# Talking-heads attention with two feed-forward layers: f32 scores by head pairs from TensorE transposes, a second mixer in quarter-array products, and one planned pool of four two-bank PSUM places

## Chip, cores, metric

The kernel runs on one core of a Trainium2 chip. The metric is the device time of one execution in microseconds, the median of several runs; the time before is 1440.85 us (three runs, 1440.46 to 1446.3).

## The reference

```python
# q, k, v: (4, 12, 448, 64) f32; w_pre, w_post: (12, 12)
scores = q @ k^T / 8                                     # per batch and head, 448 x 448
scores = einsum("bhij,hg->bgij", scores, w_pre)          # first mixer: over the heads
attn   = softmax(scores, axis=-1)
attn   = einsum("bhij,hg->bgij", attn, w_post)           # second mixer
x      = (attn @ v), heads side by side                  # 1792 x 768
h = x @ w_in;  x = (h * cos(h)) @ w_out                  # 768 -> 2048 -> 768
h = x @ w_in2; out = (relu(h) ** 2) @ w_out2             # 768 -> 2048 -> 768
```

## The kernel before

All work is recorded first, as operations of a `Plan` (L27 to L128). Each operation has the engines that may do it with a cost for each, a key from the table `KEYS`, the operations that it follows, and the buffers that it takes and gives back (`acq`, `rel`, counted in `room`). A list scheduler then fixes at build time which engine does what and in which order every engine issues; SP issues nearly all DMAs, in its own order. So a changed cost, key or buffer count moves instructions all over the program.

**Stages of a batch.** q and k come in as `raw`, 112 rows with four sequence positions each, by DMAs whose runs are 1 KB (`load_ops`, L522). Outside the first chunk their squares give norms, and the scaled values are split into two f16 halves (`x1`, `x2`, `x3`), which 16-bit DMA transposes (L629, eight a batch) bring into stacks with the head dimension on the partitions; swap copies (L639, L640) make the second stack of k. The queries are handled in chunks `CHUNKS = (0,11), (110,12), (230,12), (348,10)`: first query and number of blocks of 10 queries, 45 blocks a batch. For each chunk and head two f16 matmuls (`scores_ops`, L702) give scores in one bank `s`; ACT (L710) or DVE (L712) copies them to `sh`, and a DMA (L715) moves them into `t`, where a row is a query and a head. Only the first chunk of batch 0 takes another way: f32 transposes on TensorE (L747, L748, L772), f32 scores (L796) and moves by L824.

**A pair of blocks** then goes through the mixers (22 pairs and one single block a batch, 88 steps in all). First mixer, L874: 5 queries of 12 heads are 60 rows, so each block is two quarter products of 64x64 weights with 448 columns, the pair four quarters, in a two-bank place `m`. DVE takes the row maxima of both (L882), ACT the exponential of each block with its row sum (L890), then POOL and DVE the reciprocals (L902). For each block `g` is the block-diagonal weight matrix times the reciprocals, 128x120 (ACT L250 or DVE L248). Second mixer, L924: for each block four products, each with 112 keys of the exponentials as weights and the 120 columns of `g`, into one bank `po`, which ACT (L945) or DVE (L947) copies to `at`, keys on the partitions. After a chunk the value product (L995) multiplies `at` by v, 48 matmuls of 112 rows in two column halves, in `po` banks too; L1018 and L1029 keep the result as a sum of two 16-bit parts.

PSUM is divided into one bank for `s`, two places of two banks for `m`, and three banks for `po` (`PSB`), which the feed-forward layers use as well: gemm 1 (L1334, `h_a`) puts two of three column groups into an `m` place and the third into a `po` bank.

A name in the rows is a buffer of the program (`s`, `m`, `po`, `av` as above, `tk` and `tq` the transposes of the first chunk, `h_a` gemm 1 of the first layer).

## Time and profile before

| what | value |
|---|---|
| median of three runs | 1440.85 us |
| profiled execution, its time | 1443.57 us |
| profiled execution, its span | 1441.8 us |
| PE (TensorE matmul) busy | 1335.2 us, 93% |
| DVE busy | 959.8 us, 67% |
| ACT busy | 764.4 us, 53% |
| POOL busy | 451.3 us, 31% |

The span runs from the first to the last instruction of the profiled execution; 1.8 us of its time lie outside. The profiled execution is 2.7 us above the median. Shares are of the whole span; the stages differ much in them, and the rows below go by stage. An f32 product shows as two records in the rows, an f16 product and a transpose as one. PEclk is the mean clock granted to TensorE, as a share of its full speed.

### The profile page before, as it was taken

The page shows a single profiled execution, that of the slowest core. Times are in us where ns is not written, and L with a number is a line of the kernel's source. Part 1 is how long each engine was busy: PE and PEld are TensorE (multiplying, and loading weights), DVE is VectorE, ACT ScalarE, POOL GpSimd, SP SyncE. Part 2 cuts the span into 40 slices and gives each one's busy share as a digit, 9 for nine tenths or more (in the row PEclk, how much of TensorE's full clock was granted, in tenths as well). Part 3 has the DMA queues.
Part 4 walks back from the last instruction along what each step waited for, and adds up shares of the span by engine and source line. Part 5 has one row for each costly group of instructions (what it writes and reads, how often), then busy time and mean ns, then how long its engine had stood idle before and what let it go on. Part 6 is the DMA issues. An engine that isn't in the chain of part 4 may idle for free.

```text
span 1441.8 us, 26180 instructions
## 1 busy us (share of the span) xinstructions
PE 1335.2 (93%) x10025; PEld 886.0 (61%) x10025; DVE 959.8 (67%) x1968; ACT 764.4 (53%) x1602; POOL 451.3 (31%) x443
## 2 busy tenths in 40 slices
PE   7679888998988999998999999999986999999998
PEld 4356655765766765554455555556864976986965
DVE  5478757665668879987996886988983460461510
ACT  5478677767657747655543543654752440450620
POOL 5023102401401115632642552556361240140300
PEclk7789998999999999999899999999998999999999
DMA  8958884974757558231224133177973440541501
GB/s 170 240 166 215 199 211 143 191 175 132 153 140 196 164 204 215 59 80 53 83 83 132 61 95 125 63 220 224 333 232 117 164 144 23 168 161 44 189 17 28
DMA packets 184445, 209.51 MB, mean 145 GB/s; under 512 B 50828, under 2 KB 165888, under 8 KB 183296
## 3 DMA queue, kind: packets, MB, share of 16 engines
q1 hardware_dynamic: 184224, 207.82, 50.8%
q8 instruction: 79, 1.29, 0.4%
q14 instruction: 46, 0.38, 0.1%
q0 software_dynamic: 96, 0.01, 0.0%
HBM read 123.48 MB, written 29.10 MB: 106 GB/s over the span
## 4 chain that ended last, share of the span: by engine, by line
PE 71%; DVE 12%; DMA 7%; ACT 4%; issue 3%; POOL 1%; SPq 1%; ACTq 0%; DVEq 0%; POOLq 0%
PE h_a L1334 15%; PE o L1920 14%; PE y L1434 12%; PE h_b L1725 8%; PE po L924 7%; PE m L874 4%; DMA t<-sh 4%; PE hx_b L1725 3%; PE s L702 3%; PE av L995 3%; DMA rawin<-in_moe_w_in 2%; DVE mx L882 1%; DVE raw L258 1%; DVE raw L338 1%; ACT e L890 1%
## 5 line engine op out<-in xcount | busy, mean ns | idle before, releaser
L1434 PE MATMUL y<-g,wout 128*128 128x448 f16 x1152 | 225.5, 355 | 4.4 <-ACT g L1345 2.3
L1334 PE MATMUL h_a<-x,win 128*128 128x448 f16 x1152 | 223.9, 354 | 0.5 <-DVE k L1406 0.5
L1725 PEld LDWEIGHTS <-win 128*128 128x128 f16 x2016 | 194.9, 99 | 17.4 <-issue 15.1
L1920 PE MATMUL o<-wout,g 128*128 128x384 f16 x1152 | 191.8, 328 | 0.1
L924 PEld LDWEIGHTS po<-g,e 128*112 128x112 f32 x1440 | 163.1, 179 | 30.3 <-ACT g L250 8.2
L1434 PEld LDWEIGHTS <-wout 128*128 128x128 f16 x1152 | 112.8, 99 | 109.1 <-issue 7.5
L924 PE MATMUL po<-g,e 128*112 128x120 f32 x1440 | 171.7, 271 | 7.1 <-ACT g L250 4.1
L1334 PEld LDWEIGHTS <-win 128*128 128x128 f16 x1152 | 112.8, 99 | 105.3 <-issue 3.6
L1920 PEld LDWEIGHTS <-g 128*128 128x128 f16 x1152 | 113.5, 99 | 74.2 <-issue 2.4
L702 PE MATMUL s<-k,q 128*120 128x448 f16 (+2 forms) x360 | 108.7, 386 | 29.2 <-ACT sh L710 19.5
L1725 PE MATMUL h_b<-win 128*128 128x224 f16 x1152 | 123.9, 261 | 4.2 <-DVE win L1750 4.1
L890 ACT ACTIVATE e<-m,mx 128x448 f32<-128x448 f32 x180 | 112.2, 633 | 23.8 <-DVE mx L882 22.9
L882 DVE TENSOR_REDUCE mx<-m 128x2 f32<-128x896 f32 (+1 forms) x92 | 97.0, 1065 | 39.7 <-PE m L874 38.8
L1936 DVE SCALAR_TENSOR_TENSOR ob<-o,cols,raw 128x384 f32<-128x384 f32 x28 | 17.2, 616 | 147.8 <-PE o L1920 147.8
L874 PE MATMUL m<-t,kmix 64*64 64x448 f32 x704 | 93.0, 615 | 13.6 <-ACT e L890 8.3
L897 POOL TENSOR_SCALAR rs<-sm 128x2 f32<-128x2 f32 (+1 forms) x72 | 16.6, 231 | 283.8 <-ACT e L890 237.5
L1750 DVE TENSOR_TENSOR win<-h_b,win 128x224 f32<-128x224 f32 x128 | 48.6, 389 | 72.0 <-PE h_b L1725 50.1
L702 PEld LDWEIGHTS <-q 128*120 128x120 f16 (+2 forms) x360 | 41.6, 136 | 84.5 <-issue 77.7
L1892 POOL TENSOR_TENSOR r<-r 128x448 f32<-128x448 f32 x25 | 24.1, 964 | 198.3 <-ACT r L1769 198.2
L995 PE MATMUL av<-at,v 112*64 112x120 f32 (+2 forms) x1536 | 80.5, 262 | 5.6 <-ACT at L945 2.7
L995 PEld LDWEIGHTS av<-at,v 112*64 112x64 f32 x1536 | 74.2, 137 | 15.3 <-ACT at L945 5.4
L1350 POOL TENSOR_TENSOR g<-k,g 128x448 f16<-128x448 f32 x52 | 63.4, 1227 | 55.4 <-ACT g L1345 34.0
(310 smaller groups left out, 2225.1 us busy)
## 6 DMA issues: line engine op xcount, KB each, us to landing
win<-wp SPq DMA_DIRECT2D x32, 768.0 KB
raw<-in_moe_w_out SPq DMA_DIRECT2D x21, 1024.0 KB
t<-sh SPq DMA_DIRECT2D x96, 210.0 KB
win<-wp SPq DMA_DIRECT2D x32, 576.0 KB
raw<-in_moe_w_in SPq DMA_DIRECT2D x16, 768.0 KB
wp<-raw SPq DMA_DIRECT2D x8, 1344.0 KB
t<-sh SPq DMA_DIRECT2D x48, 192.5 KB
t<-sh SPq DMA_DIRECT2D x48, 175.0 KB
```

What stands on the lines that cost most here:

```text
L702: PE.matmul(ps[:m, :S], lhsT=lt, rhs=stacks["k"][z][:, h], start=(z == 0), stop=(z == 1))
L874: PE.matmul(st.ps[64 * x : 64 * x + 64, r, :S], lhsT=km[rows, 64 * r : 64 * r + 64], rhs=t[rows, st.blk[x]], start=True, stop=True,)
L882: DVE.tensor_reduce(st.mx[:, :n], st.ps[:, :n, :S], axis=AX.X, op=ALU.max, negate=True)
L890: ACT.activation(st.e[:, x], st.ps[:, x, :S], AF.Exp, bias=st.mx[:, x : x + 1], accum_out=st.sm[:, x : x + 1],)
L924: PE.matmul(o, lhsT=st.e[:, x, c], rhs=st.g[:, x], start=True, stop=True)
L995: PE.matmul(ps[64 * x : 64 * x + 64, gp * 120 : gp * 120 + n], lhsT=v32[:CP, g, jc * D : (jc + 1) * D], rhs=ao[:CP, jc, g, :n], start=(jc ...
L1334: PE.matmul(hb[nm, x], lhsT=t_["win"][:, x, wh, c, :], rhs=xt[b][:, c, xh], start=(c == 0 and wh == 0 and xh == 0), stop=(c == NCC - 1 and ...
L1350: (POOL if e == "POOL" else DVE).tensor_tensor(t_["g"][:, f, 1], box["k"], t_["g"][:, f, 0], op=ALU.subtract)
L1434: PE.matmul(box["ps"][:, :S], lhsT=t_["wo1"][m // 3][:, wh, f, (m % 3) * P : (m % 3 + 1) * P], rhs=t_["g"][:, f, gh], start=(f == 0 and wh ...
L1725: PE.matmul(box[at], lhsT=wt[:, k % 4, wh, c, :], rhs=y(c, xh), start=(first and c == 0 and wh == 0 and xh == 0), stop=(c == HC - 1 and wh ...
L1750: DVE.tensor_tensor(box["s"][:, to], box[at], box["s"][:, k], op=ALU.add)
L1920: PE.matmul(box["ps"][:, :HD], lhsT=(t_["g"][:, f, gh, t0 : t0 + P] if t0 + P <= S else rest()[:, f, gh]), rhs=t_["wo2"][:, 6 * hf : 6 * h ...
```

## The change

- **Loads.** q and k of a batch come by pairs of heads, the two heads of a pair side by side, in runs of 256 bytes (`load_ops`, L533, L535): 24 DMAs in batch 0, 16 in the others. v is padded to 128 rows and comes in eight DMAs (L558).
- **Transposes.** Norms, f16 halves, DMA transposes and swaps are gone, and the special first chunk too. For each pair of heads TensorE does eight f32 transposes (L580) into a two-bank place `tr`, and ACT (L590) or DVE (L592) copies 896 columns into `qk`.
- **Scores.** For each chunk and pair of heads two f32 matmuls of 64 rows, one in each row half of the array (L647), one copy of 896 columns (L655, L657), two moves (L661).
- **Second mixer.** For a pair of blocks 28 products of 64x64 weights and 60 columns, each in a quarter of the array (L747): 5 queries of 12 heads are kept apart, so the zero half of the block-diagonal `g` is not multiplied, and a pair's `g` is one multiplication (L733). Keys come in seven groups of 64, and one instruction (L775, L777) copies a pair's result to `at`.
- **Value product.** Per chunk 72 products over 128 keys and 24 over the last 64, in one two-bank place (L836, L846). The moving operand is read with a stride of five f32 elements.
- **PSUM.** One pool of four two-bank places; the planner assigns the place (`plan.slots["m"]`). Transposes, scores, both mixers, value product and the feed-forward layers all take from it, with a limit of two places on the first mixer (`pm`) and on the pairs of gemm 1 (`h`). Gemm 1 takes pairs throughout.
- **Keys.** All of `KEYS` changes; `SLOTS` spreads the pieces of w_in over three buffers.

```diff
--- before.py
+++ after.py
     KEYS = {
-        "pm": (-188.38, -3899.06, 1478.43, -349.17),
...
+        "pm": (-2.47, -3.04, -3.36, -2.62),
-    PSB = (1, 3)
-    SLOTS = (1, 2, 1, 2, 1, 2, 1, 2, 2, 2, 0, 0, 0, 0, 0, 0)
+    SLOTS = (1, 2, 3, 1, 2, 3, 2, 3, 2, 3, 2, 3, 3, 3, 0, 0)
...
-    ps_s = ctx.enter_context(tc.tile_pool(name="ps_s", bufs=PSB[0], space=PSUM))
-    ps_m = ctx.enter_context(tc.tile_pool(name="ps_m", bufs=2, space=PSUM))
-    ps_o = ctx.enter_context(tc.tile_pool(name="ps_o", bufs=PSB[1], space=PSUM))
+    ps_m = ctx.enter_context(tc.tile_pool(name="ps_m", bufs=1, space=PSUM))
...
+    plan.slots["m"] = list(range(4))
...
+    def banks(nm):
+        i = plan.now["slot"]["m"]
+        return ps_m.tile([P, 2, 512], F32, tag=f"m{i}", name=nm)
     def bank(nm):
-        return ps_o.tile([P, 512], F32, tag="po", name=nm)
+        return banks(nm)[:, 0]
...
+        def load_ops(b, key, step, seq=()):
+            last, done = seq, []
+            for hp in range(0, NP, step):
+                outs = []
+                for nm, src in (("q", q), ("k", k)):
+                    parts = [(z, c) for z in range(2) for c in (range(NC4) if step > 1 else [None])]
+                    for z, c in parts:
+                        def go(e, nm=nm, src=src, z=z, c=c, hp=hp):
+                            if (b, nm) not in raw:
+                                raw[b, nm] = new_raw((b, nm)).rearrange(
+                                    "p (h c x) -> p h c x", h=NP, c=NC4
+                                )
+                            to = raw[b, nm][:CP, hp : hp + step, :, 64 * z : 64 * z + 64]
+                            hs = src[b, 2 * hp + z : 2 * (hp + step) : 2].rearrange(
+                                "h (p c) d -> p h c d", c=NC4
+                            )
+                            if c is None:
+                                SP.dma_start(out=to[:, 0], in_=hs[:, 0])
+                            else:
+                                SP.dma_start(out=to[:, :, c], in_=hs[:, :, c])
...
+        def value_loads(b, key, seq=()):
...
-        def transpose_ops(b, nm, key, dkey, norm):
...
-                def turn(e, g=g):
-                    SP.dma_start_transpose(
-                        out=stacks[nm][0][:, 3 * g : 3 * g + 3].rearrange(
-                            "p h (c x) -> p (h c) x", x=CP
-                        ),
-                        in_=box[g][:CP].rearrange("p h x -> p (h x)"),
-                    )
-                    stage.append(box["n", g])
-                def swap(e, g=g):
-                    t, o = (x[:, 3 * g : 3 * g + 3] for x in stacks[nm])
-                    SP.dma_start(out=o[0:D], in_=t[D:P])
-                    SP.dma_start(out=o[D:P], in_=t[0:D])
...
+        qk = stk.tile([P, NP, 2, S], F32, name="qk")
+        def turn_ops(b, keys, loads):
+            outs, last = [], None
+            for hp in range(NP):
+                box = {}
+                def turn(e, hp=hp, box=box):
+                    ps = box["ps"] = banks(f"tr{b}_{hp}")
+                    for i, nm in enumerate("qk"):
+                        for c in range(NC4):
+                            PE.transpose(
+                                ps[:, i, c * CP : (c + 1) * CP], raw[b, nm][:CP, hp, c],
+                                ident[:CP, :CP],
+                            )
+                    if hp == NP - 1:
+                        raw_done((b, "q"))
+                        raw_done((b, "k"))
+                def keep(e, hp=hp, box=box):
+                    if e == "ACT":
+                        ACT.activation(qk[:, hp], box["ps"][:, :, :S], AF.Copy)
+                    else:
+                        DVE.tensor_copy(qk[:, hp], box["ps"][:, :, :S])
                 last = add(
...
-        def scores_ops(b, ch, h, key, stacked, before):
+        def scores_ops(b, ch, hp, key, turned, before):
             i0, nb = CHUNKS[ch]
             m = nb * IB
             box = {}
             def mm(e):
-                if h == 0:
+                if hp == 0:
                     tt[b, ch] = tts[ch % 2]
-                ps = ps_s.tile([P, 512], F32, tag="s", name=f"s{b}_{ch}_{h}")
-                box["ps"] = ps
-                lt = stacks["q"][0][:, h, i0 : i0 + m]
+                ps = box["ps"] = banks(f"s{b}_{ch}_{hp}")
                 for z in range(2):
+                    r = slice(64 * z, 64 * z + 64)
                     PE.matmul(
-                        ps[:m, :S], lhsT=lt, rhs=stacks["k"][z][:, h], start=(z == 0), stop=(z == 1)
+                        ps[:m, z, :S], lhsT=qk[r, hp, 0, i0 : i0 + m], rhs=qk[r, hp, 1],
+                        start=True, stop=True,
                     )
...
-        def first_chunk_ops(key, dkey, loads):
...
-            def postmix(x):
-                def go(e):
-                    if st.blk[x] == 0:
-                        at[b, ch] = atp.tile([P, 4, H, 12 * IB], F32, tag="at", name=f"at{b}_{ch}")
-                    ps = bank(f"po{st.nm}_{x}")
-                    for jc in range(4):
-                        c = slice(jc * CP, (jc + 1) * CP)
-                        o = ps[:CP, jc * HB : (jc + 1) * HB]
-                        PE.matmul(
-                            o, lhsT=st.e[:, x, c], rhs=st.g[:, x], start=True, stop=True
...
+            W = HB // 2
+            def postmix(e):
+                if st.blk[0] == 0:
+                    at[b, ch] = atp.tile([P, 7, H, 60], F32, tag="at", name=f"at{b}_{ch}")
+                ps = st.po = banks(f"po{st.nm}")
+                def product(rows, bank_, c, at_, r, jt):
+                    PE.matmul(
+                        ps[64 * c : 64 * c + 64, bank_, at_ : at_ + W],
+                        lhsT=st.e[64 * rows : 64 * rows + 64, r, 64 * jt : 64 * jt + 64],
+                        rhs=st.g[64 * rows : 64 * rows + 64, r], start=True, stop=True,
+                    )
+                if n == 2:
+                    for r in range(2):
+                        for jc in range(3):
+                            for x in range(2):
+                                for c in range(2):
+                                    product(x, x, c, (3 * r + jc) * W, r, 2 * jc + c)
+                    for x in range(2):
+                        for r in range(2):
+                            product(x, x, r, 6 * W, r, 6)
...
-            def mm(g0, ng):
-                def go(e):
-                    ao = at[b, ch]
-                    ps = bank(f"av{b}_{ch}_{g0}")
-                    for gp in range(ng):
-                        for jc in range(4):
+            def mm(e):
+                ao = at[b, ch]
+                ps = box["ps"] = banks(f"av{b}_{ch}")
+                def out(gp, x, r):
+                    return ps[64 * x : 64 * x + 64, r, gp * w : (gp + 1) * w]
+                for gp in range(NP):
+                    for jc in range(3):
+                        for r in range(2):
                             for x in range(2):
-                                g = 2 * (g0 + gp) + x
+                                g = 2 * gp + x
                                 PE.matmul(
-                                    ps[64 * x : 64 * x + 64, gp * 120 : gp * 120 + n],
-                                    lhsT=v32[:CP, g, jc * D : (jc + 1) * D],
-                                    rhs=ao[:CP, jc, g, :n],
-                                    start=(jc == 0), stop=(jc == 3),
+                                    out(gp, x, r), lhsT=v32[:, g, jc * D : (jc + 1) * D],
+                                    rhs=ao[:, 3 * r + jc, g, :w].rearrange("p (k m) -> p m k", m=HI),
+                                    start=(gp + jc == 0), stop=False, skip_group_check=True,
                                 )
...
+                for gp in range(NP):
                     for r in range(2):
...
-            if f % 3 == 1:
+            if f % 2:
                 return None
-            fs = [f] if f % 3 or f == NF - 1 else [f, f + 1]
...
-            return add("PE", 3400 * len(fs), key, go, deps, acq=["po" if f % 3 else "m"])
+            return add("PE", 3400 * len(fs), key, go, deps, acq=["m", "h"])
```

Two places of the order that follows from it. The first is PE's, in batch 0, while the second chunk goes through the mixers and the third chunk's scores are made. The digits in a name are batch, chunk, pair, and for `po` before the block; xN counts equal instructions in a row. Before:

```order
L924 MATMUL po0_1_1_0_1015<-g0_1_1_995,e0_1_1_952 112x120 x4
L924 MATMUL po0_1_1_1_1026<-g0_1_1_995,e0_1_1_952 112x120 x4
L702 LDWEIGHTS q0_180
L702 MATMUL s0_2_9_1036<-k0_181,q0_180 120x448
L702 LDWEIGHTS q0_180
L702 MATMUL s0_2_9_1036<-k1_182,q0_180 120x448
L874 MATMUL m0_1_4_1041<-t1_119,kmix0_382 64x448 x4
L874 MATMUL m0_1_5_1052<-t1_119,kmix0_382 64x448 x4
```

And the changed kernel's PE at the same place, where the scores are named by their pair of heads:

```order
L747 MATMUL po0_1_0_915<-g0_1_0_889,e0_1_0_759 64x60 x28
L647 MATMUL s0_2_5_953<-qk_152 120x448 x2
L701 MATMUL m0_1_4_962<-t1_113,kpre_111 64x448 x4
L747 MATMUL po0_1_1_970<-g0_1_1_893,e0_1_1_767 64x60 x28
L701 MATMUL m0_1_5_1006<-t1_113,kpre_111 64x448 x4
L747 MATMUL po0_1_2_1016<-g0_1_2_903,e0_1_2_884 64x60 x28
L647 MATMUL s0_3_0_1048<-qk_152 100x448 x2
L580 MATMUL tr1_0_1058<-ident_69,raw1q_345 128x112 x4
L580 MATMUL tr1_0_1058<-ident_69,raw1k_369 128x112 x4
```

A pair's second mixer is one stretch of 28 small products where two stretches of four stood, the scores have no weight loads written apart, and the transposes of the next batch's pairs now stand between them on PE.

The second place is SP's queue at the start, from its ninth row on, with the DMAs that the first chunk (`t0`) needs. Before:

```order
L629 DMA_TRANSPOSE q0_180<-x2_66 128x12x112
L824 DMA t0_118<-sh00_0_262 10x11x448
L629 DMA_TRANSPOSE k0_181<-x2_66 128x12x112
L824 DMA t0_118<-sh00_0_262 10x11x448
L629 DMA_TRANSPOSE q0_180<-x2_66 128x12x112
L629 DMA_TRANSPOSE k0_181<-x3_67 128x12x112
L824 DMA t0_118<-sh00_1_324 10x11x448 x2
L639 DMA k1_182<-k0_181 64x1344
L640 DMA k1_182<-k0_181 64x1344
```

The changed kernel's SP queue, from its seventeenth row on:

```order
L533 DMA raw0k_167<-in_k 112x4x64 x2
L558 DMA v32_109<-in_v 112x12x64
L558 DMA v32_109<-in_v 16x12x64
L558 DMA v32_109<-in_v 96x12x64
L558 DMA v32_109<-in_v 32x12x64
L558 DMA v32_109<-in_v 80x12x64
L558 DMA v32_109<-in_v 48x12x64
L558 DMA v32_109<-in_v 64x12x64
L661 DMA t0_112<-sh0_0_4_295 10x11x448 x2
L558 DMA v32_109<-in_v 64x12x64
L319 DMA x1_65<-in_moe_w_in 128x6x256
L661 DMA t0_112<-sh0_0_5_319 10x11x448 x2
```

The transposes and swaps that stood between the moves are gone; the loads of q and k (24 of them, the last ones seen here) and seven pieces of v now stand ahead of the last four of the twelve moves.

## Rows read from the trace of the kernel before

**Rows 1.** Busy time of each engine (with instructions) by stretches of the span.
```profile
core 0: us, PE busy (x) PEld busy (x) DVE busy (x) ACT busy (x) POOL busy (x), PEclk, DMA share, GB/s
0.00:58.40 58.40, 38.73 (x187) 22.49 (x187) 26.07 (x66) 24.53 (x46) 19.19 (x26) 0.77 0.89 188
58.40:531.00 472.60, 422.26 (x4042) 298.81 (x4044) 341.12 (x822) 337.34 (x854) 101.45 (x145) 0.95 0.69 174
531.00:1441.80 910.80, 874.17 (x5802) 564.70 (x5798) 592.62 (x1080) 402.58 (x702) 330.62 (x272) 0.98 0.40 127
550.00:1000.00 450.00, 439.33 (x2339) 230.16 (x2338) 381.26 (x637) 236.04 (x373) 222.94 (x172) 0.98 0.35 106
```

**Rows 2.** Waits of PE, 58.4 to 531 us: total, times, longest (us).
```profile
PE s L702 <- ACT sh L710: 17.9, 20, 2.7
PE m L874 <- ACT e L890: 8.3, 9, 1.9
```

**Rows 3.** Instruction groups, 58.4 to 531 us: busy us, mean ns | idle before, releasers.
```profile
L924 PE MATMUL po<-g,e 128*112 128x120 f32 x1440 | 171.7, 271 | 7.1 <-ACT g L250 4.1 <-DVE g L248 1.3 <-DVE at L947 0.6
...
L874 PE MATMUL m<-t,kmix 64*64 64x448 f32 x352 | 92.6, 614 | 13.6 <-ACT e L890 8.3 <-DMA t<-sh 4.7 <-issue 0.5
...
L702 PE MATMUL s<-k,q 128*120 128x448 f16 x178 | 55.9, 399 | 25.1 <-ACT sh L710 16.6 <-DVE sh L712 7.5 <-DVE mx L882 0.7
...
L995 PE MATMUL av<-at,v 112*64 112x120 f32 x768 | 42.5, 268 | 2.0 <-DVE at L947 1.7 <-ACT at L945 0.3
...
L702 PE MATMUL s<-k,q 128*100 128x448 f16 x96 | 26.8, 361 | 0.6 <-DVE sh L712 0.4
...
L702 PE MATMUL s<-k,q 128*110 128x448 f16 x72 | 21.1, 376 | 1.3 <-ACT sh L710 1.3
...
L995 PE MATMUL av<-at,v 112*64 112x110 f32 x384 | 19.8, 260 | 2.4 <-ACT at L945 1.3 <-ACT x L500 0.8 <-DVE at L947 0.4
...
L995 PE MATMUL av<-at,v 112*64 112x100 f32 x344 | 16.3, 251 | 1.1 <-ACT at L945 1.1
```

**Rows 4.** Timeline, 250 to 275 us: start, busy us, engine, line, tile, records.
```profile
251.09 0.15 PEld L874 LDWEIGHTS m<-t,kmix 64*64 64x64 f32 x4 [0.22 <-issue]
...
252.84 3.50 PE L995 MATMUL av<-at,v 112*64 112x120 f32 x64
...
256.78 0.21 PEld L874 LDWEIGHTS m<-t,kmix 64*64 64x64 f32 x8 [0.34 <-issue]
256.78 0.98 PE L874 MATMUL m<-t,kmix 64*64 64x448 f32 x8
...
269.22 1.80 PE L924 MATMUL po<-g,e 128*112 128x120 f32 x16
```

**Rows 5.** Timeline of PE, 0 to 62 us: a group of transposes, the first premix.
```profile
25.00 0.96 PE L772 MATMUL tk<-ident,raw0k 112*128 112x112 f32 x8
...
58.45 3.26 PE L874 MATMUL m<-t,kmix 64*64 64x448 f32 x16 [4.24 <-DMA t<-sh]
```

**Rows 6.** DMA, 0 to 12 us: packets, MB, share of 16 engines.
```profile
q1 hardware_dynamic: 2423, 2.38, 89.2%
```

**Rows 7.** DMA, 20 to 36 us: sizes of all packets; q1 as in rows 6.
```profile
DMA packets 7980, 2.93 MB, mean 183 GB/s; under 512 B 7454, under 2 KB 7850, under 8 KB 7978
...
q1 hardware_dynamic: 7978, 2.90, 105.6%
```

**Rows 8.** Groups of the engines behind the first mixer and the scores.
```profile
L890 ACT ACTIVATE e<-m,mx 128x448 f32<-128x448 f32 x180 | 112.2, 633 | 23.8 <-DVE mx L882 22.9 <-DVE ein L231 0.2
L882 DVE TENSOR_REDUCE mx<-m 128x2 f32<-128x896 f32 x88 | 94.6, 1085 | 39.7 <-PE m L874 38.8
...
L890 ACT ACTIVATION_READ_ACCUMULATOR e<-m,mx 128x1 f32 x180 | 36.8, 204 | 0.0
...
L710 ACT ACTIVATE sh<-s 120x448 f32<-120x448 f32 x52 | 28.2, 542 | 27.9 <-PE s L702 17.0 <-DMA t<-sh 6.3 <-issue 2.6
```

**Rows 9.** Gemm 1 of the first feed-forward layer, the page's costliest groups.
```profile
L1334 PE MATMUL h_a<-x,win 128*128 128x448 f16 x1152 | 223.9, 354 | 0.5 <-DVE k L1406 0.5
```

More of the change, by code (lines that the diff above doesn't have):

```diff
@@ new lines, in value_loads, with go @@
+        def value_loads(b, key, seq=()):
+            outs, last, at_ = [], seq, 0
+            src = v[b].rearrange("h (p c) d -> p c h d", c=NC4)
+            parts = []
+            while at_ < S:
+                n = min(P - at_ % P, CP - at_ % CP)
+                parts.append((at_ % P, at_ // P, at_ % CP, at_ // CP, n))
+                at_ += n
+            parts.append((64, 3, CP - 64, 3, 64))
+            for p0, jc, t0, c, n in parts:
+                def go(e, p0=p0, jc=jc, t0=t0, c=c, n=n):
@@ L720, in scores_ops @@
             o = add(
-                "PE", 380, key, mm, stacked[h // 3] + [before],
-                acq=["s"] + (["t"] if h == 0 else []),
-                rel=[f"{nm}{h // 3}" for nm in "qk"] if ch == 3 and h % 3 == 2 else [],
+                "PE", 760, key, mm, [turned[hp], before],
+                acq=["m"] + (["t"] if hp == 0 else []), rel=[f"qk{hp}"] if ch == 3 else [],
             )
             l = add(
-                {"ACT": 460, "DVE": 570}, 0, key, copy, [o], acq=["sh"], rel=["s"], alone=True
+                {"ACT": 950, "DVE": 1060}, 0, key, copy, [o], acq=["sh"], rel=[("m", o)], alone=True
@@ L853, in attention @@
+            return o, [
+                add("SP", 850, key, move(z), [l], rel=["sh"] * z, dma=10 * m) for z in range(2)
+            ]
         at = {}
@@ new lines, in mixed, with copy @@
+            def mixed(e):
+                ao, i = at[b, ch], st.blk[0] * HI
+                def copy(to, x):
+                    if e == "ACT":
+                        ACT.activation(to, x, AF.Copy)
+                    else:
+                        DVE.tensor_copy(to, x)
+                if n == 2:
+                    copy(
+                        ao.rearrange("p q g i -> p (q g) i")[:, :, i : i + IB].rearrange(
+                            "p a (x m) -> p x a m", x=2
+                        ),
+                        st.po[:, :, : 7 * W].rearrange("p x (a m) -> p x a m", m=HI),
+                    )
+                else:
+                    copy(
+                        ao[:, :6].rearrange("p (r q) g i -> p r (q g) i", r=2)[:, :, :, i : i + HI],
+                        st.po[:, :, : 3 * W].rearrange("p r (a m) -> p r a m", m=HI),
+                    )
+                    for r in range(2):
+                        h = slice(64 * r, 64 * r + 64)
+                        copy(
+                            ao[h, 6, :, i : i + HI],
+                            st.po[h, r, 3 * W : 4 * W].rearrange("p (a m) -> p a m", m=HI),
+                        )
@@ new lines, in view, with got, hi, lo @@
+            def view(z):
+                return xt[b][:, :, z, i0 : i0 + n].rearrange("p g (r i) -> p r g i", r=2)
+            def got():
+                return box["ps"][:, :, : NP * w].rearrange("p r (g i) -> p r g i", g=NP)
+            def hi(e):
+                ACT.activation(view(0), got(), AF.Copy, scale=inv_v[b][:, 0:1])
+            def lo(e):
+                for x in range(2):
+                    DVE.scalar_tensor_tensor(
+                        view(1)[:, x], got()[:, x], inv_v[b][:, 0:1], view(0)[:, x],
+                        op0=ALU.mult, op1=ALU.subtract,
+                    )
@@ L1046, in spaced @@
+            o = add(
+                "PE", 4900, key, mm, [before] + lows + vready[0] + x_free[b], acq=["m"],
+                rel=["at"] + (["v"] if ch == 3 else []),
+            )
+            h = add("ACT", 850, key + 0.1, hi, [o] + vready[1])
+            x_fin[b].append(add("DVE", 1100, key + 0.15, lo, [h], rel=[("m", o)], alone=True))
+            return o
         def spaced(nm, n):
```

626 lines of the change are left out of this document (192 added, 434 removed).

## The prediction

> **What bounds the kernel now.** I read first the busy time of each engine stretch by stretch [rows 1]. Up to 58.4 us TensorE computes for 38.7 us at a mean clock of 0.77 while the DMA engines are 89% busy: the kernel is being loaded. From 58.4 to 531 us, the rest of attention, PE is busy for 422.3 of 472.6 us (89%), DVE and ACT for 341 and 337 (72% each), the DMA engines 69%. From 531 us on, the two feed-forward parts, PE is busy for 874 of 911 us (96%). So past the start PE is the bound, and a change has to shorten its work. What PE waits for in attention is small and scattered: its largest two waits are 17.9 and 8.3 us out of 50 [rows 2]. The groups of PE's work in that stretch [rows 3] say where its time is: the second mixer (L924) 171.7 us, the first mixer (L874) 92.6, the scores (L702) 55.9 + 26.8 + 21.1 = 103.8, the value product (L995) 42.5 + 19.8 + 16.3 = 78.6. They sum to 446.7 against 422.3 us busy, since neighbouring matmuls overlap; I carry the ratio 0.945 along.
>
> **How long a small f32 matmul lasts.** This price carries the sum. An f32 product stands in the rows as two records. Sixteen records of L924 (120 columns, 112 of 128 rows) take 1.80 us, and eight of L874 (448 columns, four 64x64 quarters of the array at once) take 0.98 us [rows 4]. One f16 record of 448 columns lasts 0.36 to 0.40 us [rows 3]; eight such one after another would be 3 us. So the four quarters run side by side, and 0.98 is two passes: 0.37 to the start of the second, and the 0.61 that a record lasts. L924's records last 0.27 us; with the last one off, the other fifteen go by (1.80 - 0.27) / 15 = 102 ns each at 120 columns, thus about 53 ns at 60. The value product's 64 records, alternating between two column halves, take 3.50 us: 54.7 ns a record, half of 109, so two at a time also works there.
>
> **The change part by part, steady attention.** *Second mixer.* Now per pair of blocks 8 products, 16 records in series. Then 28 quarter products of 60 columns, 56 records in seven rounds of four, each two passes: 14 x 53 ns + 0.27 = 1.01 us. Seen from the weight loads: eight of them at 64x64 take 0.21 us and four 0.15 [rows 4], so 15 ns for one more, and 56 x 15 + 0.27 = 1.1 us. I take 1.0 us, times 88 pairs = 88 us in place of 171.7. *First mixer.* The same, 92.6. *Scores.* Two f16 products of 448 columns per head go, two f32 products in two row halves per pair of heads come. Their shape is that of L874's rows (two passes of 448 columns, side by side), so 0.98 us; 84 of the 96 fall in this stretch: 82 us for 103.8. *Transposes on PE.* New: 8 per pair of heads; eight f32 ones take 0.96 us in the start [rows 5]. 18 of the 24 pairs (batches 1 to 3): 17 us. *Value product.* 72 products of 60 columns on all rows and 24 on quarters per chunk; by the rate above 72 x 53 ns (two at a time, two passes) + 12 x 53 + 0.27 = 4.7 us, at av's own 54.7 ns 4.9; 16 chunks: 78 us, as now. Sum 88 + 92.6 + 82 + 17 + 78 = 358, times 0.945 = **338 us** instead of 422.3.
>
> *How much of that the span sees.* At today's share of 89% the stretch would last 380 us. But before, scores, first mixer and second mixer had places of their own in PSUM (1 + 2x2 + 3 banks); now all share four of two banks. One pair's stay there: first mixer 0.98 (PE) + 1.09 (row maximum) + 2 x (0.63 + 0.20) (exponential and its sum) [rows 8] = 3.74 us; its share of scores 0.98 + 2 x 0.54 = 2.06; second mixer 1.0 + about 1.0 for its copy; transposes 0.4, value product 1.25 by their share: together 9.5 us, over four places 2.4 us of a pair's 423 / 88 = 4.8 us. Half full on average, so no bound by itself, but a premix holds its place through two other engines, and its limit of two places stays. ACT and DVE lose work: 88 multiplications for g, one a pair, instead of 180, one a block, no squares, norms and halves of q and k; they gain 24 copies of 896 columns (the copies of scores keep their columns). They hide these; at 72% of a stretch that becomes a tenth shorter, with less in it, they stay covers, not bounds. The moves (L661) carry the same bytes. I take a PE share of 80%: 338 / 0.80 = 423, **-50 us**, with ends of 89% (380) and 72% (470).
>
> **The start.** The first premix runs at 58.45 us, waiting for a move [rows 5]. Gone from the road to it are the scalings, the 16-bit transposes and the swaps on SP's queue. But q and k of batch 0 now come in 2 x 5376 packets of 256 bytes instead of 1 KB. In the first 12 us 2423 packets at 89.2% of 16 engines cost 71 ns each, nearly all of 1 KB [rows 6]; between 20 and 36 us 7978, nearly all under 512 bytes, at a full share 34 ns each [rows 7]. So a 256-byte packet costs between 18 ns (a quarter of 71) and 34: q and k 12 to 23 us. On the same queue, ahead of the last moves, lie v (6144 packets: 7 to 13), twelve moves of 192.5 KB at the 188 GB/s of the start [rows 1]: 12, and the first piece of w_in 4. That is 35 to 52 and 4 us of latency, as that wait shows: 39 to 56. I take 45, a little under the middle since rows 7's stretch held transposes too: **-13 us** (-19 to -2).
>
> **Feed-forward.** The order is nearly the same; gemm 1 loses its third bank pool and takes pairs in two places. Today it idles 0.5 us over 1152 matmuls [rows 9], so there is nothing to gain, and DVE is 85% busy there (381 of 450 us [rows 1]) and hides less when places run short. I take **+6 us**, from 0 to +30.
>
> **Sum.** -13 - 50 + 6 = -57 on the profiled execution's 1443.6 us, so 1386.6; it lies 2.7 above the median of the runs, so **1384 us**. The likeliest case's own range runs from 1350 (share 86%, start -13, no loss behind) to 1412 (share 75%).
>
> **Rivals.** Where PE's work grows by some us, I put the stretch midway between today's idle 85 us staying on top (338 / 0.8 - 338) and the share of 89% coming back.
>
> *The records don't pass four at a time; slower.* For: no row has four quarters at 60 columns, and the nearest row with so short an interval is av's 54.7 ns a record. Against: the weight loads' 15 ns. At 54.7 a pair takes 3.06 us, more than today's 1.95 (171.7 / 88). At 45 ns: 2.52 us, +1.52 x 88 x 0.945 = 126 us of work, 464; midway between 549 and 521 = 535 us, total 1496. Slower than before begins where the pair takes 1.89 us, at 34 ns a record. Chance 0.08.
>
> *They pass two at a time.* As in av: 14 pairs x 2 passes x 53 ns + 0.2 = 1.68 us, +57 us of work, 395: midway of 444 and 480 = 462, total 1423. Beside it stands the Trainium skill, "TensorE: Matmul & The Clock Gate", section "Wait — 56ns, not 53.3ns?": start-to-start of matmuls never falls below about 25 ns. By that an estimate would be 56 x 25 = 1.4 us a pair, between this case and mine. No row of before shows such a start-to-start for matmuls. Chance 0.12.
>
> *The strided operand costs.* The value product now reads its columns five f32 apart. No row shows such a read by PE. If it doubled the passes, 72 x 54.7 ns = +3.9 us x 16 x 0.945 = 59 us, the same end: 1425. The Trainium skill, "SBUF — State Buffer", section "Specifications (TRN2)", says for this that lines are of 16 bytes and full bandwidth needs two hits in a line; 20 bytes apart there is one. Chance 0.08.
>
> *The four places bind.* A chain of pair after pair through PE, DVE, ACT and back holds PE at 72%: 470 us, total 1431. For: PE's waits today are already for copies out of PSUM [rows 2]. Chance 0.12.
>
> *Feed-forward loses 30 us to shared places.* 1408. Chance 0.05.
>
> **How the numbers follow.** The forecast has 0.55. About 0.5% (7 us) is what a measurement can tell from no change. Every case but the first rival ends under 1433.6; but of the 0.32 of the three near it I take 0.08 as no change and 0.04 as slower, as two may come together. So faster 0.80, same 0.08, slower 0.12. Low 1340 is a share of 87% (389 us) with the start at -19 and feed-forward at 0; high 1434 takes in all rivals but the first.
>
> **What would show it.** First premix near 45 us. The second mixer's group of 56 records at 1.0 us a pair: 14 ns start to start. Scores at 0.98 us each pair. A value chunk of 4.9 us; 8.7 would be the strided read. PE busy for about 338 us in steady attention, at 80%; waits for exponentials and for copies out of PSUM now at its head. Attention's end near 470 us instead of 531, and from there on about 917 us. I am wrong if the second mixer isn't under 1.5 us a pair, or if PE falls to 72% in attention.

## The result and the profile after

The changed kernel takes 1452.41 us (median of five runs, 1451.38 to 1454.65) against 1443.18 for the kernel before on the same chip: ratio 1.0067, 95% interval 1.0047 to 1.0086. It is slower by about 9 us where 57 less were forecast. Its profiled execution has a span of 1449.9 us, 8.1 more than before.

The busy times by stretch, cut at the first premix (the first mixer's first product), the first `h_a`, the last `y` (gemm 2 of the first feed-forward layer, "layer 1" below) and the end, with the columns of [rows 1]:

```profile
0.00:48.90 48.90, 28.61 (x126) 14.25 (x127) 15.36 (x35) 17.70 (x24) 13.53 (x18) 0.77 0.90 184
48.90:518.00 469.10, 428.51 (x9374) 299.39 (x9375) 292.52 (x533) 256.08 (x548) 71.24 (x166) 0.97 0.61 163
...
518.10:1010.30 492.20, 459.11 (x2384) 237.14 (x2383) 398.63 (x685) 252.17 (x389) 206.31 (x161) 0.97 0.34 104
1010.30:1449.90 439.60, 420.42 (x3374) 329.33 (x3372) 189.19 (x397) 151.23 (x311) 96.12 (x91) 0.98 0.39 131
```

The kernel before, cut at the same events:

```profile
58.40:533.30 474.90, 424.56 (x4083) 300.70 (x4083) 342.37 (x828) 338.08 (x856) 101.45 (x145) 0.95 0.69 176
...
533.30:993.90 460.60, 450.80 (x2378) 233.91 (x2375) 385.23 (x646) 240.09 (x377) 221.96 (x172) 0.99 0.38 116
993.90:1441.80 447.90, 421.07 (x3383) 328.91 (x3380) 206.16 (x430) 161.74 (x324) 108.66 (x100) 0.98 0.41 138
```

So the start gives 9.5 us, steady attention 5.8, layer 2 8.3; layer 1 takes 31.6 more. And in attention PE isn't idle: it is busy for 428.5 of 469.1 us (91%), a little more than before. Its work didn't shrink. The groups of that stretch say which part (with the copies out of the second mixer, L775 and L777, for experiment 1):

```profile
L747 PE MATMUL po<-g,e 64*64 64x60 f32 x5040 | 98.4, 225 | 19.6 <-issue 10.4 <-ACT at L775 3.6 <-ACT e L717 1.5
L701 PE MATMUL m<-t,kpre 64*64 64x448 f32 x352 | 91.5, 600 | 9.8 <-ACT sh L655 5.9 <-ACT at L775 1.9 <-ACT e L717 1.6
...
L836 PE MATMUL av<-at,v 128*64 128x60 f32 x1152 | 65.9, 292 | 0.8 <-ACT at L775 0.8
L775 ACT ACTIVATE at<-po 128x840 f32<-128x840 f32 x51 | 49.3, 970 | 61.5 <-PE po L747 61.0
...
L777 DVE COPY at<-po 128x840 f32<-128x840 f32 x37 | 38.0, 1030 | 14.3 <-PE po L747 14.2
...
L836 PE MATMUL av<-at,v 128*64 128x55 f32 x576 | 30.8, 283 | 0.4 <-issue 0.2
L836 PE MATMUL av<-at,v 128*64 128x50 f32 x576 | 27.9, 274 | 0.0
...
L846 PE MATMUL av<-at,v 64*64 64x60 f32 x384 | 12.4, 289 | 0.0
```

The second mixer fell from 171.7 to 98.4 us [rows 3]. The value product rose from 78.6 to 148 (65.9 + 30.8 + 27.9, and 23.5 in quarter products). The timeline of PE shows one chunk of it, and one pair of the second mixer:

```profile
261.29 8.23 PE L836 MATMUL av<-at,v 128*64 128x60 f32 x144 [0.77 <-ACT at L775]
269.46 1.54 PE L846 MATMUL av<-at,v 64*64 64x60 f32 x48
...
273.76 1.04 PE L747 MATMUL po<-g,e 64*64 64x60 f32 x56 [0.15 <-ACT sh L655]
```

144 records in 8.23 us are 57 ns each at 60 columns, where [rows 4] had 54.7 at 120: either the two column halves no longer run side by side, or every pass takes twice as long. The 48 quarter records are slow as well: 1.54 us, where the prediction's rate gives 12 x 0.053 + 0.27 = 0.9. The 56 records of the second mixer go by at nearly the forecast rate.

Layer 1 is longer mainly because PE idles: 33.1 us there (492.2 - 459.1) against 9.8 before (460.6 - 450.8). Waits of PE after attention (total, times, longest), first the changed kernel:

```profile
PE n_l L301 <- DVE k L1217: 5.7, 1, 5.7
PE n_in L272 <- DVE k L1217: 4.8, 1, 4.8
PE n_in L281 <- DVE ard_in L278: 4.3, 3, 2.4
...
PE n_out L301 <- ACT raw L351: 3.3, 2, 2.8
...
PE lx_x L1118 <- DVE k L1217: 2.1, 1, 2.1
PE h_a L1145 <- DVE k L1217: 1.9, 2, 1.4
```

```profile
PE y L1434 <- ACT g L1345: 2.3, 1, 2.3
PE n_y L276 <- DVE ard_y L273: 2.3, 1, 2.3
...
PE h_a L1334 <- DVE k L1406: 0.5, 1, 0.5
```

The names `n_...` are small products that give the norms of weights and inputs. `DVE k` (L1217, L1406) is the step that reads gemm 1's result for the last time and so frees its PSUM place: 14.5 us of the idle time are waits for it.

### The profile page after: what moved, and what is told of

It reads as the page before. It is cut to its first block, busy times and chain, and to the rows that moved or that the text cites. A ratio compares the mean times of both kernels' runs of the same rounds, so it can differ in the third digit from the quotient of the medians.

```text
span 1449.9 us, 35787 instructions
## 1 busy us (share of the span) xinstructions
PE 1336.8 (92%) x15255; PEld 880.1 (61%) x15255; DVE 895.8 (62%) x1647; ACT 677.3 (47%) x1271; POOL 387.2 (27%) x436
## 4 chain that ended last, share of the span: by engine, by line
PE 66%; DVE 14%; DMA 6%; issue 5%; ACT 5%; SPq 3%; POOL 2%; ACTq 0%; DVEq 0%; POOLq 0%
PE o L1738 15%; PE y L1245 9%; PE h_b L1541 9%; PE av L836 8%; PE h_a L1145 6%; PE po L747 5%; PE m L701 4%; PE hx_b L1541 4%; PE s L647 4%; DMA t<-sh 3%; DVE raw L337 1%; PE av L846 1%; DVE raw L343 1%; DVE raw L263 1%; DMA raw<-in_moe_w_out 1%
## 5 line engine op out<-in xcount | busy, mean ns | idle before, releaser
L1145 PE MATMUL h_a<-x,win 128*128 128x448 f16 x1152 | 228.7, 359 | 5.1 <-DVE eout L236 2.6
L747 PEld LDWEIGHTS po<-g,e 64*64 64x64 f32 x5040 | 92.1, 140 | 59.9 <-issue 40.0
L836 PEld LDWEIGHTS av<-at,v 128*64 128x64 f32 x2304 | 120.8, 155 | 10.2 <-ACT at L775 6.5
L836 PE MATMUL av<-at,v 128*64 128x60 f32 (+2 forms) x2304 | 124.6, 285 | 1.1 <-ACT at L775 0.8
L747 PE MATMUL po<-g,e 64*64 64x60 f32 x5040 | 98.4, 225 | 19.6 <-issue 10.4
L647 PE MATMUL s<-qk 64*120 64x448 f32 (+2 forms) x384 | 94.4, 591 | 9.9 <-ACT sh L655 4.7
L701 PE MATMUL m<-t,kpre 64*64 64x448 f32 x704 | 92.4, 600 | 9.8 <-ACT sh L655 5.9
L1209 POOL TENSOR_TENSOR u<-u,k 128x448 f32<-128x448 f32 x43 | 59.9, 1403 | 88.9 <-DVE k L1204 88.6
L775 ACT ACTIVATE at<-po 128x840 f32<-128x840 f32 (+2 forms) x57 | 50.9, 899 | 62.4 <-PE po L747 61.9
L657 DVE COPY sh<-s 120x896 f32<-120x896 f32 (+2 forms) x44 | 47.7, 1086 | 42.0 <-PE s L647 33.3
```

The source lines that it names most:

```text
L647: PE.matmul(ps[:m, z, :S], lhsT=qk[r, hp, 0, i0 : i0 + m], rhs=qk[r, hp, 1], start=True, stop=True,)
L701: PE.matmul(st.ps[64 * x : 64 * x + 64, r, :S], lhsT=km[rows, 64 * r : 64 * r + 64], rhs=t[rows, st.blk[x]], start=True, stop=True,)
L747: PE.matmul(ps[64 * c : 64 * c + 64, bank_, at_ : at_ + W], lhsT=st.e[64 * rows : 64 * rows + 64, r, 64 * jt : 64 * jt + 64], rhs=st.g[64 ...
L775: ACT.activation(to, x, AF.Copy)
L836: PE.matmul(out(gp, x, r), lhsT=v32[:, g, jc * D : (jc + 1) * D], rhs=ao[:, 3 * r + jc, g, :w].rearrange("p (k m) -> p m k", m=HI), start= ...
L1145: PE.matmul(hb[nm, x], lhsT=t_["win"][:, x, wh, c, :], rhs=xt[b][:, c, xh], start=(c == 0 and wh == 0 and xh == 0), stop=(c == NCC - 1 and ...
```

## Experiments

**1. Is it the stride?** In the first kernel the copy out of the second mixer writes `at` query-major and the value product reads its columns contiguously. The order of operations is that of the change, since the planner's numbers are untouched.

```diff
+                ao = at[b, ch][:, :, :, : nb * HI].rearrange("p q g (m k) -> p (q g) m k", k=nb)
...
-                        ao.rearrange("p q g i -> p (q g) i")[:, :, i : i + IB].rearrange(
-                            "p a (x m) -> p x a m", x=2
-                        ),
+                        ao[:, :, :, k0 : k0 + 2].rearrange("p a m x -> p x a m"),
...
-                                    rhs=ao[:, 3 * r + jc, g, :w].rearrange("p (k m) -> p m k", m=HI),
+                                    rhs=ao[:, 3 * r + jc, g, :w],
```

> The copy out of the second mixer writes each chunk query-major, so the value product reads its 60 columns contiguously; same products, same instruction counts. Theory S (the operand read five f32 apart doubles each pass): 144 records of the value product fall from 8.2 to about 4.0 us a chunk, the 48 quarter records from 1.5 to about 0.8; 16 chunks x 4.9 = 78 us of PE work gone, at PE's share of 91% some 70 to 85 us: 1370 to 1385 us. Rival Q (products over 128 rows in the two column halves don't run side by side as those over 112 rows did): 57 ns a record stays, 1452 us within 0.5%. Rival W (the copies with scattered writes get slower and become the bound): the records halve but the copies rise from 0.9 us and the time falls by less than 40.

1426.06 us, ratio to before 0.987 (0.984 to 0.990). The groups, value product and copy on ACT and on DVE:

```profile
L776 ACT ACTIVATE at<-po 128x840 f32<-128x840 f32 x51 | 84.7, 1669 | 61.7 <-PE po L747 60.8
...
L778 DVE COPY at<-po 128x840 f32<-128x840 f32 x37 | 60.7, 1651 | 16.3 <-PE po L747 15.8
...
L835 PE MATMUL av<-at,v 128*64 128x60 f32 x1152 | 35.5, 223 | 2.8 <-ACT at L776 1.8 <-issue 0.9
```

S holds for PE: 65.9 us became 35.5, and Q is out. But S's time, 1370 to 1385, was missed. W holds in part: the copy with jumps of 40 to 48 bytes between f32 costs 1.67 us where the change's cost 0.97 on ACT, and the time falls by only 26 us. That the copies are the bound isn't shown: in experiment 3 they cost what they did in the change, and only 9 us come of it.

The chunks have 60, 55 or 50 columns. A chunk's 144 records take the same here with 60 and with 50:

```profile
439.93 4.42 PE L835 MATMUL av<-at,v 128*64 128x60 f32 x144
...
483.12 4.41 PE L835 MATMUL av<-at,v 128*64 128x50 f32 x144
```

So from 50 to 60 columns the time of a contiguous product doesn't go with its columns: 29.4 ns from start to start, (4.42 - 0.22) / 143, thus 59 in each column half, where the prediction took about 53 from 102 at 120 columns.

**2. From which step on?** The 60-column chunks read with another step in each batch, and so other columns than the product needs.

```diff
+                def col(h, q, g):
+                    sd = b + 1
+                    if w < 60:
+                        return ao[h, q, g, :w].rearrange("p (k m) -> p m k", m=HI)
+                    g = min(g, H - sd)
+                    return ao[h, q, g : g + sd, 0 : 60 : sd]
...
-                                    rhs=ao[:, 3 * r + jc, g, :w].rearrange("p (k m) -> p m k", m=HI),
+                                    rhs=col(slice(0, P), 3 * r + jc, g),
```

> In the chunks with 60 columns the value product reads wrong columns with a step of 1 f32 in batch 0, 2 in batch 1, 3 in batch 2, 4 in batch 3 (the output is then not the reference's); the other chunks keep their step of 5. Theory S: 144 records take about 4 us with step 1 and 8.2 with step 5, and the steps between show where it begins (by 16-byte lines with two hits wanted: step 2 like step 1, steps 3 and 4 towards 5). Rival Q: 8.2 us at every step.

The timeline; the chunks of 60 columns are, in this order, of step 1, 2, 3 and 4, those of 50 and 55 columns have kept step 5:

```profile
116.80 4.42 PE L843 MATMUL av<-at,v 128*64 128x60 f32 x144
...
166.72 6.95 PE L843 MATMUL av<-at,v 128*64 128x50 f32 x144
...
218.77 4.41 PE L843 MATMUL av<-at,v 128*64 128x60 f32 x144
...
336.69 6.24 PE L843 MATMUL av<-at,v 128*64 128x60 f32 x144
...
410.07 7.63 PE L843 MATMUL av<-at,v 128*64 128x55 f32 x144
...
462.23 8.17 PE L843 MATMUL av<-at,v 128*64 128x60 f32 x144
```

Steps 1 and 2 cost the same, 3 costs 1.41 times as much, 4 (8.17 us) about as much as 5 in the change (8.23). With step 5 the time does go with the columns: 6.95, 7.63 and 8.23 us for 50, 55 and 60. That step 2 costs nothing is shown only for products this short, whose contiguous time doesn't go with the columns. The Trainium skill, "SBUF — State Buffer", section "Specifications (TRN2)", has lines of 16 bytes that want two hits each: steps 1 and 2 have them, 4 and 5 have one. The trace agrees, with 4.42 and 4.41 us against 8.17 and 8.23.

**3. Where to put the permutation.** Once in the value product's last copies, which read PSUM with step 5 (two ACT and ten DVE instructions a chunk); once in the second mixer's copy again, but with the two blocks of the pair innermost, so that two adjacent f32 are written in turn. The latter was run twice. Its edit against the kernel of experiment 1:

```diff
-  ao[:, :, :, k0 : k0 + 2].rearrange("p a m x -> p x a m"),
-  st.po[:, :, : 7 * W].rearrange("p x (a m) -> p x a m", m=HI),
+  ao[:, :, :, k0 : k0 + 2],
+  st.po[:, :, : 7 * W].rearrange("p x (a m) -> p a m x", m=HI),
```

> The value product reads contiguously and the permutation moves to the last copies: the result's high half is two ACT instructions a chunk that read PSUM with a step of five, the low half ten small DVE ones; the second mixer's copies go back to 0.97 us. Order of operations as in the change. Theory S: 8.2 us become 4.4 a chunk as in the run before; the copies no longer cost 0.65 us more each, and the time falls below that of the scattered copies, 1395 to 1415 us. Rival L (what is left after the stride is taken away isn't the copies but waits in the order as planned): 1420 to 1430, like the scattered copies.

> As the scattered copies, but the copy out of the second mixer goes through the two blocks innermost, so that two adjacent f32 are written one after the other, while PSUM is read from alternating banks. If the price of the scattered write is one per 48-byte jump, the copy falls from 1.67 us towards 1.3; if reading PSUM in jumps costs as much, it stays at 1.6 or rises.

> The pair-wise copy again, now timed: about 1415 us, 2% under before, as in its one look; if that look was lucky, up to 1426 as with the scattered copies.

The first takes 1419.54 us (0.984, 0.982 to 0.986), between S's 1395 to 1415 and L's 1420 to 1430. The second takes 1415.43 in a single run and 1417.35 in several (0.982, 0.978 to 0.986). Its copies and its stretches, cut as above:

```profile
L776 ACT ACTIVATE at<-po 128x840 f32<-128x840 f32 x51 | 48.4, 952 | 62.8 <-PE po L747 62.4
...
L778 DVE COPY at<-po 128x840 f32<-128x840 f32 x37 | 38.2, 1036 | 15.6 <-PE po L747 15.4
```

```profile
50.70:478.70 428.00, 374.72 (x9375) 242.44 (x9376) 294.56 (x536) 256.01 (x548) 71.74 (x166) 0.95 0.67 180
478.70:974.00 495.30, 462.94 (x2384) 238.17 (x2383) 398.62 (x683) 251.73 (x388) 206.80 (x161) 0.96 0.34 102
974.00:1413.00 439.00, 419.21 (x3374) 328.37 (x3372) 188.62 (x397) 151.31 (x311) 97.00 (x91) 0.98 0.39 132
```

Writing pairs of adjacent f32 takes the price off whole: 952 ns, where about 1.3 us was the better of the two expectations. Without the stride steady attention lasts 428 us, 47 less than before; the forecast was 423. PE's 54 us less of work (428.5 to 374.7) gave 41 of the stretch, since its idle time rose from 40.6 to 53.3. The feed-forward layers still take 934 us against 908.5 before.

**4. The planner's knowledge, and the fillers.** With the strided operand, the planner is told the measured cost, and in another kernel the filler matmuls are left out.

```diff
-  "PE", 4900, key, mm, [before] + lows + vready[0] + x_free[b], acq=["m"],
+  "PE", 9760, key, mm, [before] + lows + vready[0] + x_free[b], acq=["m"],
```

```diff
-    WARM = (22, 6)
+    WARM = (22, 0)
```

> Only the planner's cost of a chunk's value product changes, 4900 to 9760 ns, what it was measured to take. Theory S: the work is the same, so 1452 us within 8. Rival P (the order was planned for a value product half as long, and the loss is misplaced instructions): waits in attention shrink and the time falls by 15 us or more.

> The 30 filler matmuls at attention's end are left out (6 us of PE work). If they lie in idle time, as I think, the time stays within 3 us, or rises where the clock falls in the gap; rival: they stand ahead of needed work on PE and cost 4 to 6 us, 1446 us.

1489.11 us (1.031, 1.030 to 1.033) and 1475.12 (1.022, 1.020 to 1.023): no expectation held. Both edits make a new order, the first from batch 0 on, the second from attention's end on, and the kernels took 37 and 23 us more than the change. In both, layer 1 got longer and layer 2 shorter (by the last value product and the last `y`: 532 and 527 us for 494, 422 and 420 for 439). Neither says anything of its own subject.

**5. Is layer 1 slower for its shared PSUM places?** When attention is over, pools of one bank, two pairs and three banks replace the four places, and the layers are recorded as before the change; then the same with the old keys of these layers; then with three places in attention.

```diff
+  def other_pools(e):
+      psx.close()
+      for nm, n in (("s", 1), ("m", 2), ("o", 3)):
+          PB[nm] = ctx.enter_context(tc.tile_pool(name=f"ps_{nm}2", bufs=n, space=PSUM))
```

> The pair-wise copy, and the feed-forward layers recorded as before the change (gemm 1 in a pair and a single, norms in a bank of their own), in PSUM pools of one bank, two pairs and three banks that replace the four places when attention is over; keys as in the change. Theory R (layer 1 lost its 32 us to the shared places): layer 1, from the first h_a to the last y, falls from 496 to about 465 us and the time to about 1385. Rival K (it lost them to the retuned order, or to DVE and ACT being late for reasons that don't hang on places): layer 1 stays at 490 or more, 1410 to 1420.

> As the run before it, with the two rows of keys that only the feed-forward layers use (w2, wo) as before the change too. Theory R: like the run before it within 8 us. Rival K: layer 1 falls to about 465 us only here, and layer 2 goes from 439 to 448: about 1395.

> As the kernel with the old feed-forward layers in pools of their own, but attention has three places of two banks instead of four (the others stay empty). By the prediction's count (2.4 us of use per place in a 4.8-us pair) three places are 65% full: attention takes up to 15 us more. Rival D (the places bind): attention takes 40 us more or worse.

1442.67 us (0.9995, 0.997 to 1.002), 1445.75 (1.0025, 1.000 to 1.005) and 1491.16 in a single run: neither R's 1385 nor K's 1410 to 1420, and the old keys change nothing beyond 3 us. The first kernel's three stretches, and the third's attention:

```profile
50.40:486.70 436.30, 382.64 (x9374) 247.36 (x9374) 288.95 (x535) 254.16 (x546) 71.07 (x164) 0.93 0.66 175
486.70:958.20 471.50, 452.77 (x2367) 234.41 (x2368) 365.55 (x624) 223.49 (x355) 205.47 (x161) 0.97 0.27 84
958.20:1448.00 489.80, 427.45 (x3390) 333.47 (x3388) 226.71 (x461) 175.47 (x336) 111.59 (x104) 0.95 0.43 142
```

```profile
49.70:530.70 481.00, 397.05 (x9378) 247.78 (x9379) 298.33 (x543) 264.47 (x556) 60.61 (x142) 0.93 0.60 162
```

Layer 1 fell by 24 us, as R has it, but layer 2 rose by 51: there PE now waits 35.2 us for squares of raw weights (`n_l` for ACT's `raw`). The weights' preparation had moved from layer 1 to layer 2, with the order: DVE, ACT and POOL have 198 instructions on `raw` in layer 2, where the change has 136. With three places attention takes 45 us more, as D has it, though the prediction's count had them 65% full. That a place less binds isn't shown by itself: the order was planned anew for three places, and PE's waits there are scattered.

**6. Waits for late norms.** PE's waits in layer 1 stand mostly ahead of small norm products. Here the planned order is kept, but each of these is issued one large PE operation later, in the kernel with pair-wise copies and in the first kernel of 5.

```diff
+            j = next((j for j in range(i + 1, len(log)) if log[j][1] == "PE" and not log[j][0]["late"]), None)
+            if j is not None and log[j][2] < end + 160:
+                log.insert(j + 1, log[i])
+                del log[i]
```

> The kernel with pair-wise copies; the planned order is kept, but each small norm matmul of the feed-forward layers (one to two columns, for the scales of weights and of x and y) is issued one large PE operation later. Theory H (PE stands in order behind small norm matmuls whose inputs ACT and DVE deliver later than planned, 25 us of layer 1's 32 idle): those waits fall under 8 us, layer 1 goes from 495 to 470 or 480 us, the time from 1417 to 1395 to 1405. Rival B (ACT and DVE set the pace; the waits move to h_a, y and h_b): layer 1 stays at 488 or more, 1410 to 1420.

> The same shift of the norm matmuls in the kernel with the old feed-forward layers in their own pools, where layer 2 waited 35 us at norm matmuls for the squares of raw weights. Theory H: 1443 falls by 15 us or more. Rival B (the weights' preparation itself is late): layer 2 keeps its 490 us, 1438 to 1446.

1437.8 us (0.994, 0.992 to 0.997) and 1477.17 (1.024, 1.019 to 1.028): slower by 20 and 34 us than the kernels they start from. H is refuted. Part of the loss is that a norm that comes later makes the scales later that depend on it: in the first kernel gemm 1's waits for the scale `eout` went from 1.8 to 4.0 us. The rest isn't traced.

**7. Places alone, then order alone.** In two kernels made from the one with pair-wise copies all PSUM is one tile of eight banks. As a control (`SPLIT` false) each operation gets its pair of banks; in the second kernel (`SPLIT` true) an operation that needs one bank takes one. The order is the same in both. Against that, one planner constant changes in the kernel before and in the one with pair-wise copies, so that only the order moves, and with it which engine takes a step.

```diff
+  if one and self.SPLIT:
+      half = [i for i in free if i ^ 1 not in free]
+      return [(half or free)[0]]
```

```diff
-    LAT, DMA_START, DMA_END = 170.0, 650.0, 1000.0
+    LAT, DMA_START, DMA_END = 180.0, 650.0, 1000.0
```

> Control for the next run: the kernel with pair-wise copies, all PSUM as one tile of eight banks of which every operation gets its pair of banks as before, in the same planned order. 1417 us within 6, layer 1 about 495 us.

> The same order, but an operation that needs one bank (norms, l1 bounds, y, o) takes one and leaves the other to others, so that a bank is taken longer after it came free. Theory R (PE waits in layer 1 for places that DVE frees late): the 17 us of PE's waits for releases by the h_a chain shrink to under 6 and layer 1 falls by 10 us or more, the time to 1400 to 1408. Rival K (the order sets it, the next wait takes over): layer 1 within 5 us, 1412 to 1420.

> The kernel before, with one constant of the planner changed, the latency between engines from 170 to 180 ns; nothing else, so only the order of operations moves. Theory K (the order as tuned is worth more than any rule): the time rises by 15 to 50 us, most of it in the feed-forward layers. Rival: within 5 us of 1443.

> The same constant changed in the kernel with pair-wise copies: by theory K 1425 to 1470 with attention and feed-forward parts both moving by tens of us; rival: 1417 within 6.

1409.51 us (0.977, 0.976 to 0.979) for the control and 1409.23 (0.976, 0.974 to 0.978): the same. PE's waits from 475 to 975 us, control first (total, times, longest; the tiles are all called psum here, L297 and L318 are norm products):

```profile
PE psum L297 <- DVE ard_in L294: 11.2, 3, 7.1
PE psum L318 <- ACT raw L369: 6.4, 2, 3.8
PE psum L318 <- DVE k L1236: 4.2, 2, 2.8
```

```profile
PE psum L297 <- DVE ard_in L294: 13.0, 3, 8.0
PE psum L318 <- ACT raw L369: 12.3, 4, 3.8
```

The waits for a freed place (`DVE k`) are gone, and those for the norm's input and for the squares of raw weights have grown. Within this order the wait that ends is replaced by the next: from the kernel with pair-wise copies and four tiles over the control to single banks, PE's waits for `k` in layer 1 go from 15.6 us to 5.8 to none, its idle time there is 32.4, 32.6 and 32.4. So freeing places alone gains nothing. The order alone costs much: 1528.31 us for the kernel before and 1465.46 for the other, in a single run each, 6 and 3.4% more. The former's stretches after the start, cut at the end of the last value product, since the first pair of `h_a` stands ahead of it:

```profile
58.90:550.20 491.30, 430.02 (x4117) 303.45 (x4119) 342.59 (x847) 343.35 (x854) 93.14 (x130) 0.94 0.69 176
550.20:1011.70 461.50, 443.98 (x2338) 230.37 (x2335) 355.82 (x598) 228.09 (x361) 209.82 (x167) 0.98 0.29 87
1011.70:1526.50 514.80, 430.47 (x3390) 334.31 (x3388) 232.83 (x481) 179.31 (x341) 106.33 (x96) 0.92 0.43 139
```

With no rule changed its feed-forward layers take 976 us instead of 908.5, nearly all of the rise in layer 2. In the other kernel it is the reverse: layer 1 takes 540 us (499 with pair-wise copies, by the same cut), layer 2 424 (439).

What moves with the order is the weights' preparation. Counting the instructions of DVE, ACT and POOL on `raw` in layer 2, with the length of that layer:

| kernel | on `raw` in layer 2 | layer 2, us |
|---|---|---|
| pair-wise copies, constant changed | 104 | 424 |
| value product's cost changed (4) | 109 | 422 |
| no fillers (4) | 111 | 420 |
| the change | 136 | 440 |
| before | 160 | 448 |
| old layers and keys in own pools (5) | 184 | 486 |
| old layers in own pools (5) | 198 | 490 |
| before, constant changed | 200 | 515 |

The more of it is left for layer 2, the longer, nearly without exception, that layer, and layer 1 has the rest: 338 in the change, 313 before. No run moved it by itself.

## Why the prediction was wrong, step by step

- **Second mixer: right.** 1.04 us a pair for 1.0; 14.8 ns from start to start, (1.04 - 0.225) / 55; 98.4 us in all for 88. Both rivals on its rate fell. The floor of about 25 ns from the Trainium skill, "TensorE: Matmul & The Clock Gate", section "Wait — 56ns, not 53.3ns?", doesn't hold for quarters side by side here.
- **First mixer, scores, transposes: right.** 91.5 us for 92.6; scores 81 for 82; transposes 17.5 for 17.
- **Value product: the step that failed.** "By the rate above 72 x 53 ns (two at a time, two passes)" took the rate from contiguous reads. The step of five nearly doubles each pass: 8.23 + 1.54 = 9.8 us a chunk for 4.9, and 147 us in the stretch for 78. Even read contiguously a chunk takes 4.42 + 0.93 = 5.35 us, since a record of 50 to 60 columns starts 59 ns after the last one in its half and not 53. The mechanism stood among the rivals, with 0.08 and a stretch of 464 us (it was 469); that these are close is luck, as the rival had 397 us of work at 86% and the trace has 428.5 at 91%. It also left the quarter products at their old price: 8.7 us a chunk for 9.8. The sentence beside it, from the Trainium skill, "SBUF — State Buffer", section "Specifications (TRN2)", was the best evidence at hand, and I gave it too little, since no row of before had a strided read. Taking the stride away brought 35 us (1452.4 to 1417.4), and that decides the sign: 1417 lies under the time before. Neither of the two signs of being wrong that the prediction ends on came, only the one for the value chunk.
- **Work and PE's share in attention: both off, and by luck against each other.** With the stride away 374.7 us of work at 88% made 428 us; I had 338 at 80%, 423. Second mixer and value product came to 100.5 and 85.7 us for 88 and 78, and some 20 us of norms, fillers and the single blocks' first mixer weren't in the sum. The four places bind less than feared.
- **Start: about right,** -9.5 us for -13: the first premix ran at 48.90.
- **Feed-forward: mis-sized,** +23.3 us for +6, inside its bounds. The cause that I gave, too few places beside gemm 1, has its waits in the trace (14.5 us for `k`), but within the order as planned freeing places didn't shorten PE's idle time. An order that changes by itself moved these layers by 26 and 68 us in two single runs, the weights' preparation wandering between layer 1 and layer 2. The change has 25 instructions of it more in layer 1 than before, and 24 fewer in layer 2; that its 23 us come from this fits, but isn't shown. Which operations of its order cost them stays open.

Of the 68 us between 1384 and 1452, by the stretches, 46 lie in attention (469.1 for 423), 41 of them the stride's (469.1 against 428.0); 17 lie in the feed-forward layers and 4 in the start. The likeliest case had no term for the stride.

## What to carry to other kernels

Where a change saves copies by letting TensorE read its moving operand with a step, look at the step in bytes: at 60 columns two f32 was free here, three cost 1.41 times as much, four 1.85 times. Put the permutation into a copy that writes adjacent pairs instead. In a kernel whose order comes from a tuned scheduler, an edit is only comparable with the order held; a re-planned order alone cost 2.5 to 6% here, in three kernels (two of them run once), more than the stride.

## What was not expected of the hardware

- The copy of 128x840 f32 from PSUM costs 1669 ns on ACT and 1651 on DVE when every f32 goes 40 to 48 bytes on, and 952 and 1036 when two adjacent f32 follow each other, the same as in runs of five (970 and 1030), although PSUM is then read from two banks in turn.
- Quarter products of 64x64x60 in f32 start 14.8 ns apart, 59 in each quarter; contiguous products of 128x64 in two column halves start 29.4 ns apart, 59 in each half, at 50 columns as at 60.
- One PSUM tile of eight banks instead of four tiles of two, in the same order, took 1409.5 us for 1417.4. Why is open; PE's idle time in layer 1 is the same.
